# Windowed attention and two MLPs on one core: how the first heads are loaded, split and scored, and what TensorE does beside them

## The chip, the core and the metric

The kernel runs on one core of one Trainium2 chip. The core has TensorE (matrix products; its rows in the profile are PE, and PEld for its weight loads), VectorE (DVE), ScalarE (ACT), GpSimd (POOL) and SyncE (SP, which here issues the transfers between HBM and the on-chip memory). The metric is the time of one execution on the device in microseconds, as the median of several runs.

## The reference

Causal attention in a window of 128 positions with a slope per head, then two MLPs. Batch 4, 8 heads, 576 positions, head dimension 64; 2304 tokens of 512 columns; hidden size 2048.

```python
scores = scale * np.matmul(q, k.transpose(0, 1, 3, 2))
rel = pos[:, None] - pos[None, :]
bias = slopes[:, None, None] * (-np.abs(rel))[None, :, :]
mask = (rel >= 0) & (rel < 128)
scores = np.where(mask, scores + bias[None], -1000000000.0)
attn = softmax(scores)                       # with 1e-9 added to the sum
x = np.matmul(attn, v)                       # -> (2304, 512)
h = x @ w_in1;  x = where(h >= 1, h, where(h <= -1, 0, (h + 1)**2 / 4)) @ w_out1
h = x @ w_in2;  out = (h * np.clip(h + 3, 0, 6) / 6) @ w_out2
```

q, k and v are float32, the MLP weights float64.

## The kernel before

Products run in a rounded float32 type. For accuracy a factor is split into a rounded high part ("hi", `split_hi`) and the rest ("lo", `split_lo`), and a product is the sum of two or three partial products. Float64 weights arrive as words and are converted on the chip: `Weights.conv1` (ScalarE, two instructions), `conv2` (VectorE, three), `conv3` (ScalarE rounds, VectorE subtracts). One conversion serves one f, a slice of 128 of the 2048 hidden columns, with its w_in and w_out. `W1.load()` issues the next half (w_in, then w_out) of the next f on SP; `conv_tick` issues the second part of one conversion and the first part of the next.

The tokens are cut into nine units of 128 to 320; a unit has 8 heads, a head one step per 128 queries. Unit 0 has 256 tokens and so 16 steps, unit 1 has 320 and 24, unit 2 has 192 and 16. `tick` issues one step: `stage_a` (scores, bias and row extreme, exponential), and for earlier steps `stage_b` (transposes of the probabilities, p to t to th), `stage_c_whole` (product with v into r, normalising) and `stage_d_whole` (transpose into x, split). The first three units (`WHOLE`) take this form with unsplit probabilities; later units normalise ahead of the transposes and multiply in split form.

For each head `load` fetches keys and queries, 64 rows, twice, into both halves of the 128 partitions (kr, qr; two buffers each). `prep` splits: kh and kl hold hi and lo of the keys in both halves, and qs holds the queries' hi in its first 64 partitions and their lo in the last 64 (L286 rounds all 128 on POOL, L288 subtracts on POOL). So one product with kh over 128 rows gives hi times hi plus lo times hi, and two (L321, L322) make a score. v comes for two heads at a time, with a column of ones on either side for the row sums.

`make_consts` builds distances (rel) and a mask on POOL; `make_bias` makes each of the eight heads' bias on VectorE at the head's first step, from both. It also makes the identity for the transposes.

The program starts with `n_pre` = 20 ticks, which cover unit 0, with a load of a weight half at every third tick and a `conv_tick` at the last two. Then blocks 0 and 1 of 256 tokens each run the first half of the f (chunks of `Mlp1.first`, 12 products into h, L522, and `second`, 12 products into acc, L562), and then the second half; a hook between chunks issues weight loads, conversions and ticks of units 1 and 2 (`spread`). From then on the MLP's products fill the kernel, with the later units' steps between them.

SP issues its transfers in the order written (`manual_schedule`). For the other engines a planner chooses the order of instructions ahead of time from costs, so an engine's order can differ from the order of the code; each engine then executes its list in order.

Of the kernel before, what the change touches and what calls it, by code (L numbers as in the profile page):

```python
# [2 lines left out]

# [6 lines left out]
F32 = mybir.dt.float32  # L10
# [7 lines left out]
P = 128  # L18
# [7 lines left out]
F64_HI_TO_F32 = 2.0 ** -112  # L26


HI = dict(k="act", q="act", q_whole="pool", v="any", th="act", xf="act", x="act", g="act", x2="act")
LO = dict(k="any", q="pool", v="pool", x="any", x_whole="dve", g="pool", g_tail="dve", g2="dve", x2="dve")  # L30

LAG = 2
LAG_TAIL = 4
LAG_B, LAG_C, LAG_C_SPLIT, LAG_D = 2, 3, 4, 4
WHOLE = 3


@with_exitstack
def tile_window_attention_two_mlps(
# [53 lines left out]

    ident = const.tile([P, P], F32, tag="ident", name="ident")

    rel_mask = []

    def make_consts():
        both = cpool.tile([P, 2, PIECE], F32, tag="m", name="both")
        irel, mask = both[:, 0, :2 * P], both[:, 1, :2 * P]  # L100
        rel_mask.extend((irel, mask))

        nc.gpsimd.iota(irel, pattern=[[-1, 2 * P]], base=P, channel_multiplier=1,
                       allow_small_or_imprecise_dtypes=True)
        nc.gpsimd.memset(mask, 0.0)
        nc.gpsimd.affine_select(out=mask, in_=mask, compare_op=ALU.is_ge, fill=NEG / scale,
                                base=P, pattern=[[-1, 2 * P]], channel_multiplier=1)
        nc.gpsimd.affine_select(out=mask, in_=mask, compare_op=ALU.is_ge, fill=NEG / scale,
                                base=WINDOW - 1 - P, pattern=[[1, 2 * P]], channel_multiplier=-1)
        make_identity(nc, ident)  # L110
# [21 lines left out]
    class Weights:  # L132
# [47 lines left out]
            split_lo("dve", hl[:, 1], m, hl[:, 0])  # L180
            self.hl[f] = hl

        def conv_tick(self):
# [12 lines left out]
        def w_in(self, part, c, f):  # L196
# [5 lines left out]

    class Head:
        pass

    heads = []
    for j, (t0, n) in enumerate(units):
        for h in range(H):  # L210
            u = Head()
            u.unit, u.h, u.t0 = j, h, t0
            u.b, u.q0 = divmod(t0, S)
            u.nq = n
            u.q1 = u.q0 + n
# [5 lines left out]
            u.whole = j < WHOLE  # L221
            u.n_a = u.n_c = 0
            u.prepped = False
            heads.append(u)
# [6 lines left out]
    class Attention:  # L231
# [5 lines left out]
        def load(self, n):  # L237

            u = heads[n]
            u.kr = self.raw.tile([P, KMAX], F32, tag="kr", name=f"kr{n}")  # L240
            u.qr = self.raw.tile([P, UMAX], F32, tag="qr", name=f"qr{n}")
            self.k_owners.append(n)
            for dst, src, a, m in ((u.kr, kT, u.k0, u.nk), (u.qr, qT, u.q0, u.nq)):
                for r in range(2):
                    nc.sync.dma_start(out=dst[r * D:(r + 1) * D, :m], in_=src[u.b, u.h, :, a:a + m])
            if u.h % 2 == 0:
                self.v_owners.append(n)
                u.vt = self.raw.tile([P, KCH, 2 * D + 2], F32, tag="vr", name=f"vr{n}")
                u.vr = u.vt[:, :, 1:2 * D + 1]
                if u.whole:  # L250
# [12 lines left out]

        def may_load(self, n):

            if n >= len(heads):
                return False
            if len(self.k_owners) > 1 and not heads[self.k_owners[-2]].prepped:
                return False
            if heads[n].h % 2 == 0 and len(self.v_owners) > 1:  # L270
                o = self.v_owners[-2]
                if heads[o].whole and heads[o + 1].n_c < len(heads[o + 1].qbs):
                    return False
                if not heads[o].prepped:
                    return False
            return True

        def prep(self, n):
            u = heads[n]
            u.prepped = True  # L280
            u.kh = self.proc.tile([P, KMAX], F32R, tag="kh", name=f"kh{n}")
            u.kl = self.proc.tile([P, KMAX], F32R, tag="kl", name=f"kl{n}")
            u.qs = self.proc.tile([P, UMAX], F32R, tag="qs", name=f"qs{n}")
            m, nk = u.nq, u.nk
            split_hi(HI["k"], u.kh[:, :nk], u.kr[:, :nk])
            split_hi(HI["q_whole" if u.whole else "q"], u.qs[:, :m], u.qr[:, :m])  # L286
            split_lo(LO["k"], u.kl[:, :nk], u.kr[:, :nk], u.kh[:, :nk])
            split_lo(LO["q"], u.qs[D:, :m], u.qr[D:, :m], u.qs[D:, :m])  # L288
            if u.whole:
                return  # L290
            if u.h % 2 == 0:

                u.vs = self.proc.tile([P, 2, KCH, 2, D], F32R, tag="vs", name=f"vs{n}")
                full, rest = divmod(nk, P)
                parts = [(slice(0, P), slice(0, full))]
                if rest:
                    parts.append((slice(0, rest), slice(full, full + 1)))
                for pp, cc in parts:
                    for j in range(2):
                        src = u.vr[pp, cc, j * D:(j + 1) * D]  # L300
                        hi, lo = u.vs[pp, j, cc, j, :], u.vs[pp, j, cc, 1 - j, :]
                        split_hi(HI["v"], hi, src)
                        split_lo(LO["v"], lo, src, hi)
            else:
                u.vs = heads[n - 1].vs

        def stage_a(self, n, i):
# [21 lines left out]
            nc.scalar.activation(out=pt[:m, :nk], in_=pt[:m, :nk], func=AF.Exp, bias=sm[:m, 0:1],  # L329
                                 scale=-1.0, accum_out=None if u.whole else sm[:m, 1:2])  # L330
# [369 lines left out]
    with ExitStack() as actx:  # L700
# [3 lines left out]
        proc = actx.enter_context(tc.tile_pool(name="proc", bufs=2))  # L704
        work = actx.enter_context(tc.tile_pool(name="work", bufs=2))
        bias8 = actx.enter_context(tc.tile_pool(name="bias", bufs=1)).tile([P, H, 2 * P], BF16, tag="bias8", name="bias8")
        att = Attention(raw, proc, work, xs)

        att.more_loads(1)
        W1.load()  # L710
        make_consts()
# [12 lines left out]

        def spread(part, ticks, conv):
# [4 lines left out]
            def hook(f, after):  # L730
                k = 2 * (f - part[0]) + after + 1
                W1.load()
                while W1.n_conv < conv0 + min(conv, -(-conv * k // slots)) and W1.conv_tick():
# [122 lines left out]
```

## Time and profile before

| what | value |
|---|---|
| median of 3 runs | 1015.49 us (1014.09 to 1015.96) |
| profiled execution, its own time | 1019.89 us |
| its span, first to last instruction | 1018.1 us |
| mean granted TensorE clock over the span | 0.987 |
| TensorE (PE) busy | 984.6 us, 97% |
| VectorE (DVE) busy | 600.9 us, 59% |
| ScalarE (ACT) busy | 520.7 us, 51% |
| GpSimd (POOL) busy | 252.9 us, 25% |
| moved by DMA | 78.50 MB, mean 77 GB/s |

The median is of runs without the profiler. The profiled execution is a run of its own; its durations and windows add up to its own span. Busy shares are means over the whole span, and stages differ much.

### The profile page before, as it was taken

How to read it: one execution, taken by the hardware profiler on the slowest of the kernel's cores; microseconds unless marked ns; L12 is line 12 of the kernel's file. 1: busy time of each engine (PE TensorE's matmuls, PEld its weight loads, DVE VectorE, ACT ScalarE, POOL GpSimd, SP SyncE). 2: the span in 40 equal slices, each digit the busy share in tenths (PEclk: the TensorE clock that was granted, in tenths of full speed). 3: DMA queues.
4: the chain of work that ended last, by engine and by line, in shares of the span. 5: the costliest groups of instructions: out<-in, count | busy, mean ns of one | idle time of the engine just before them, and what ended most of it. 6: DMA issues, size and time to landing. Idle time of an engine off the chain costs nothing.

```text
span 1018.1 us, 17964 instructions
## 1 busy us (share of the span) xinstructions
PE 984.6 (97%) x6380; PEld 899.3 (88%) x6380; DVE 600.9 (59%) x1583; ACT 520.7 (51%) x1286; POOL 252.9 (25%) x398
## 2 busy tenths in 40 slices
PE   5898999999999999999999999999999999999998
PEld 4787888999989999999999999999988888888886
DVE  5778998566678676677757997922242223222222
ACT  4768875455677666566645777522242223222221
POOL 3334356444556555465410000000000000000000
PEclk9979999999999999999999999999999999999999
DMA  6565542311323211322005566000020002001001
GB/s 177 146 215 186 181 151 78 99 56 43 91 57 100 77 40 47 88 66 77 2 22 177 203 212 217 1 1 1 1 104 1 0 1 83 1 1 42 1 1 42
DMA packets 69785, 78.50 MB, mean 77 GB/s; under 512 B 7488, under 2 KB 61760, under 8 KB 69696
## 3 DMA queue, kind: packets, MB, share of 16 engines
q1 hardware_dynamic: 69696, 77.36, 24.4%
q8 instruction: 50, 0.82, 0.3%
q14 instruction: 39, 0.32, 0.1%
HBM read 66.85 MB, written 10.49 MB: 76 GB/s over the span
## 4 chain that ended last, share of the span: by engine, by line
PE 77%; DVE 4%; ACT 2%; issue 1%; POOL 1%; DMA 1%; SPq 0%; ACTq 0%; POOLq 0%
PE h L522 35%; PE acc L615 19%; PE acc L562 16%; PE r L441 2%; PE s L321 1%; PE t L355 1%; PE s L322 1%; PE t L356 1%; DVE r L549 0%; DMA rawb<-w_out 0%; DVE ma L173 0%; DVE p L326 0%; DVE r L551 0%; ACT r L550 0%; POOL g L128 0%
## 5 line engine op out<-in xcount | busy, mean ns | idle before, releaser
L522 PE MATMUL h<-x,wa 128*128 128x256 f32 x1728 | 246.2, 290 | 1.1 <-DVE wa L128 1.1
L562 PE MATMUL acc<-g,wa 128*128 128x256 f32 x1728 | 234.7, 284 | 2.0 <-POOL g L128 1.7
L522 PEld LDWEIGHTS h<-x,wa 128*128 128x128 f32 x1728 | 226.3, 197 | 2.3 <-DVE wa L128 1.5
L562 PEld LDWEIGHTS acc<-g,wa 128*128 128x128 f32 x1728 | 217.7, 191 | 3.8 <-POOL g L128 2.5
L522 PE MATMUL h<-x,wb 128*128 128x512 f32 (+1 forms) x960 | 210.5, 368 | 0.2 <-DVE r L605 0.2
L615 PE MATMUL acc<-wb,g 128*128 128x512 f32 x864 | 209.4, 390 | 0.0
L522 PEld LDWEIGHTS h<-x,wb 128*128 128x128 f32 x960 | 176.2, 188 | 25.5 <-DVE r L605 0.5
L615 PEld LDWEIGHTS acc<-wb,g 128*128 128x128 f32 x864 | 161.7, 188 | 32.4
L605 DVE SCALAR_TENSOR_TENSOR r<-r,h 128x512 f32<-128x512 f32 (+1 forms) x80 | 50.7, 634 | 201.2 <-ACT r L604 201.1
L604 ACT ACTIVATE r<-h 128x512 f32<-128x512 f32 (+1 forms) x80 | 44.5, 556 | 209.6 <-PE h L522 209.6
L121 ACT CAST g<-r 128x256 fp32r<-128x256 f32 (+2 forms) x224 | 104.3, 466 | 84.0 <-DVE r L605 49.8
L128 POOL TENSOR_TENSOR g<-r,g 128x256 fp32r<-128x256 f32 x112 | 90.4, 808 | 142.3 <-ACT g L121 128.1
L550 ACT ACTIVATE r<-r 128x256 f32<-128x256 f32 x144 | 60.0, 417 | 79.9 <-DVE r L549 76.7
L128 DVE TENSOR_TENSOR g<-r,g 128x512 fp32r<-128x512 f32 (+2 forms) x112 | 64.5, 576 | 46.8 <-ACT g L121 46.7
L329 ACT ACTIVATE p<-p,sm 128x256 f32<-128x256 f32 (+2 forms) x160 | 76.2, 477 | 23.8 <-DVE sm L326 21.7
L551 DVE TENSOR_TENSOR r<-h,r 128x256 f32<-128x256 f32 x144 | 60.6, 421 | 29.7 <-ACT r L550 28.6
L549 DVE TENSOR_SCALAR r<-h 128x256 f32<-128x256 f32 x144 | 60.3, 418 | 28.3 <-PE h L522 23.8
L128 POOL TENSOR_TENSOR qs<-qr,qs 64x256 fp32r<-64x256 f32 (+3 forms) x72 | 68.0, 946 | 24.5 <-issue 10.4
L326 DVE CUSTOM_DVE_ANT_0 p<-s,bias 128x256 f32<-128x256 f32 (+2 forms) x160 | 59.8, 375 | 21.0 <-PE s L322 20.1
L321 PE MATMUL s<-kh,qs 128*128 128x256 f32 (+2 forms) x160 | 57.1, 358 | 12.9 <-POOL qs L128 11.1
L334 POOL TENSOR_SCALAR p<-p,sm 128x256 f32<-128x256 f32 (+2 forms) x104 | 49.3, 474 | 54.2 <-DVE sm L333 35.1
L356 PE MATMUL t<-ident,p 128*128 128x128 f32 (+1 forms) x160 | 45.9, 287 | 3.5 <-ACT p L329 2.3
(71 smaller groups left out, 1112.3 us busy)
## 6 DMA issues: line engine op xcount, KB each, us to landing
rawa<-w_in SPq DMA_DIRECT2D x16, 512.0 KB, 5.3
rawa<-w_out SPq DMA_DIRECT2D x16, 512.0 KB, 5.0
rawb<-w_in SPq DMA_DIRECT2D x16, 512.0 KB, 3.7
rawb<-w_out SPq DMA_DIRECT2D x16, 512.0 KB, 4.7
x2d<-o SPq DMA_DIRECT2D x22, 256.0 KB, 2.2
kr<-kT SPq DMA_DIRECT2D x48, 112.0 KB, 2.6
out<-o SPq DMA_DIRECT2D x18, 256.0 KB, 2.2
kr<-kT SPq DMA_DIRECT2D x64, 64.0 KB, 2.2
```

The source lines that it names most:

```text
L121: nc.scalar.copy(hi, x)
L128: engines[eng].tensor_tensor(out=lo, in0=x, in1=hi.bitcast(F32), op=ALU.subtract)
L321: nc.tensor.matmul(ps[:m, :nk], u.qs[:, qo:qo + m], u.kh[:, ko:ko + nk], start=True, stop=False)
L326: nc.vector.tensor_tensor_reduce(out=pt[:m, :nk], in0=ps[:m, :nk], in1=bias8[:m, u.h, bo:bo + nk], scale=-scale, scalar=3.0e38, op0=ALU.ad ...
L329: nc.scalar.activation(out=pt[:m, :nk], in_=pt[:m, :nk], func=AF.Exp, bias=sm[:m, 0:1], scale=-1.0, accum_out=None if u.whole else sm[:m, ...
L356: nc.tensor.transpose(ps[:m, 1, :m], pt[:m, po:po + m], ident[:m, :m])
L522: nc.tensor.matmul(ps[:, :n], self.W.w_in(a, c, f), self.x_chunk(x, b, c, n), start=(k == 0), stop=(k == 3 * KC - 1))
L549: nc.vector.tensor_scalar(out=r[:, :n], in0=ps[:, :n], scalar1=-1.0, scalar2=1.0, op0=ALU.max, op1=ALU.min)
L550: nc.scalar.activation(out=r[:, :n], in_=r[:, :n], func=AF.Square, bias=0.5, scale=0.5)
L551: nc.vector.tensor_tensor(out=r[:, :n], in0=ps[:, :n], in1=r[:, :n], op=ALU.max)
L562: nc.tensor.matmul(acc[i][:, o * n:(o + 1) * n], self.W.w_out(a, f)[:, e * P:(e + 1) * P], g[:, b, :n], start=(first and k == 0 and o == 0 ...
L615: nc.tensor.matmul(acc[t][:, :DM], g[:, b, t * P:(t + 1) * P], self.W.w_out(a, f), start=(first and k == 0), stop=(last and k == 2))
```

## The change

Four things are changed in the first part of the program. In unit 0 (`PAIRS = 1`) the keys of two heads are loaded once, one head in partitions 0 to 63 and the other in 64 to 127, and so are the queries; the hi and lo parts are whole tiles (kh, kl, qh, ql), and a score is four products over 64 rows in place of two over 128. Queries are rounded on VectorE there instead of POOL. Unit 0's v goes to a tile of its own in the place of the last weight. The mask is folded into the distances, and all eight biases are made ahead of the first step, each as one product with the slope. TensorE gets products of zeros: 14 of 512 columns at the start, and one of 256 columns ahead of each score in the first three units, into the same bank, which the score then overwrites. The times at which the first ticks load and convert weights move (`LOAD_AT`, `CONV_AT`), and the planner is told to place `conv1` behind the last exponential issued and the first ticks behind the fifth bias. A copy of one zero on ScalarE comes first of all on that engine.

```diff
-HI = dict(k="act", q="act", q_whole="pool", ...)
-LO = dict(k="any", q="pool", v="pool", ...)
+HI = dict(k="act", q="act", q_pair="dve", q_whole="pool", ...)
+LO = dict(k="any", k_pair="dve", q="pool", q_pair="pool", v="pool", ...)
+WARM_UP = 14
+PAIRS = 1
+LOAD_AT = (1, 4, 7, 10, 13, 16, 19)
+CONV_AT = (9, 15)
...
+    def keep_busy(bank, n):
+        nc.tensor.matmul(bank[:, :n], zeros[:, :P], zeros[:, :n], start=True, stop=True, skip_group_check=True)
...
-        nc.gpsimd.memset(mask, 0.0)
-        nc.gpsimd.affine_select(out=mask, in_=mask, compare_op=ALU.is_ge, fill=NEG / scale,
+        nc.gpsimd.affine_select(out=rel, in_=rel, compare_op=ALU.is_ge, fill=-NEG / min(slopes),
...
-    def make_bias(h):
-        nc.vector.scalar_tensor_tensor(out=bias8[:, h, :], in0=rel_mask[0], scalar=-slopes[h] / scale,
-                                       in1=rel_mask[1], op0=ALU.mult, op1=ALU.add)
+        return [nc.vector.tensor_scalar(out=bias8[:, h, :], in0=rel, scalar1=-slopes[h] / scale, scalar2=None,
+                                        op0=ALU.mult) for h in range(H)]
...
             if n < KF:
-                self.conv1(n)
+                with tc.issue_after(after.ins) if after else nullcontext():
+                    self.conv1(n)
...
+            if not u.pair or u.h % 2 == 0:
...
+                    if u.pair:
+                        nc.sync.dma_start(out=dst[:, :m],
+                                          in_=src[u.b, u.h:u.h + 2, :, a:a + m].rearrange("h d m -> (h d) m"))
+                        continue
...
+                    if n == 0:
+                        self.first_v = wpool.tile([P, H // 2, u.nk // P, 2 * D + 2], F32, tag=f"w{KF - 1}", name="first_v")
+                        nc.gpsimd.memset(self.first_v[:, :, :, 0:2 * D + 2:2 * D + 1], 1.0)
...
+    def prep_pair(self, u, n):
...
+            split_hi(HI["k"], u.kh[:, :nk], u.kr[:, :nk])
+            split_hi(HI["q_pair"], u.qh[:, :m], u.qr[:, :m])
+            split_lo(LO["k_pair"], u.kl[:, :nk], u.kr[:, :nk], u.kh[:, :nk])
+            split_lo(LO["q_pair"], u.ql[:, :m], u.qr[:, :m], u.qh[:, :m])
+
+        def scores(self, u, ps, qo, ko, m, nk):
+            if u.pair:
+                d = slice(u.h % 2 * D, (u.h % 2 + 1) * D)
+                parts = [(q[d], k[d]) for k in (u.kh, u.kl) for q in (u.qh, u.ql)]
+            else:
+                parts = [(u.qs, u.kh), (u.qs, u.kl)]
+            for w, (q, k) in enumerate(parts):
+                nc.tensor.matmul(ps[:m, :nk], q[:, qo:qo + m], k[:, ko:ko + nk],
+                                 start=(w == 0), stop=(w == len(parts) - 1))
...
-            if n < H and i == 0:
-                make_bias(n)
...
-            nc.tensor.matmul(ps[:m, :nk], u.qs[:, qo:qo + m], u.kh[:, ko:ko + nk], start=True, stop=False)
-            nc.tensor.matmul(ps[:m, :nk], u.qs[:, qo:qo + m], u.kl[:, ko:ko + nk], start=False, stop=True)
+            if u.whole:
+                keep_busy(ps, 2 * P)
+            self.scores(u, ps, qo, ko, m, nk)
...
-        att.more_loads(1)
+        nc.vector.memset(zeros, 0.0)
+        nc.scalar.copy(zeros[:, 0:1], nc.const_aps.tensor(0.0, [P, 1], F32))
+        bank = psum.tile([P, BANK], F32, tag="h1", name="busy")
+        for _ in range(WARM_UP):
+            keep_busy(bank, BANK)
+        att.more_loads(3)
...
-            att.tick()
-            if t % 3 == 0:
+            with tc.issue_after(bias[H // 2].ins):
+                att.tick()
+            if t in LOAD_AT:
                 W1.load()
-            if t >= n_pre - 2:
-                W1.conv_tick()
+            if t in CONV_AT:
+                W1.conv_tick(att.exp)
```

## Rows read from the trace of the kernel before

**Rows 1.** Windows by stage: busy us (instructions) by engine, clock, DMA share, GB/s.

```profile
core 0: us, PE busy (x) PEld busy (x) DVE busy (x) ACT busy (x) POOL busy (x), PEclk, DMA share, GB/s
0.00:9.40 9.40, 0.00 (x1) 0.01 (x1) 2.70 (x6) 2.09 (x3) 3.77 (x16) 1.00 0.41 117
9.40:43.30 33.90, 29.62 (x122) 25.68 (x123) 24.14 (x67) 22.03 (x49) 9.81 (x18) 1.00 0.59 171
43.30:46.70 3.40, 2.48 (x16) 1.75 (x15) 3.33 (x10) 2.49 (x5) 1.43 (x3) 1.00 0.73 230
46.70:63.80 17.10, 16.67 (x75) 14.40 (x74) 8.32 (x30) 9.61 (x26) 4.19 (x7) 0.50 0.70 209
63.80:91.10 27.30, 24.20 (x176) 20.27 (x174) 24.98 (x58) 22.17 (x53) 12.83 (x13) 1.00 0.59 190
91.10:110.60 19.50, 17.37 (x112) 15.45 (x113) 16.59 (x43) 15.08 (x34) 6.51 (x9) 0.85 0.43 124
...
180.00:538.00 358.00, 352.95 (x2904) 344.27 (x2904) 249.70 (x896) 222.46 (x706) 175.82 (x293) 1.00 0.21 60
...
680.00:1018.10 338.10, 334.22 (x1515) 281.68 (x1513) 95.33 (x146) 85.90 (x148) 0.00 (x0) 1.00 0.06 21
```

**Rows 2.** Groups of TensorE's instructions, 10 to 41 us: count, busy us, mean ns.

```profile
L322 PE MATMUL s<-kl,qs 128*128 128x256 f32 x8 | 3.7, 460 | 0.0
```

**Rows 3.** The same, 47 to 63.5 us.

```profile
L322 PE MATMUL s<-kl,qs 128*128 128x256 f32 x5 | 2.1, 415 | 0.0
```

**Rows 4.** The same, 180 to 400 us.

```profile
L322 PE MATMUL s<-kl,qs 128*128 128x256 f32 x46 | 12.8, 279 | 0.0
```

**Rows 5.** Chain of waits, late in unit work: start us, us, what.

```profile
522.14 4.45 PE acc L562 x36
```

**Rows 6.** Timeline of the first 10 us: start us, us, engine, what.

```profile
0.73 1.20 SPq L245 DMA_DIRECT2D kr<-kT  x2
...
3.59 1.28 ACT L121 ACT_TABLE_LOAD   x1 [3.59 <-DMA kr<-kT]
...
8.57 1.64 POOL L128 TENSOR_TENSOR qs<-qr,qs 64x256 fp32r<-64x256 f32 x2
...
9.40 0.47 PE L321 MATMUL s<-kh,qs 128*128 128x128 f32 x1 [9.40 <-POOL qs L128]
```

**Rows 7.** Timeline of SP, 44 to 110 us.

```profile
50.59 0.58 SPq L154 DMA_DIRECT2D rawa<-w_out  x1
```

**Rows 8.** Timeline of ScalarE, 45 to 67 us.

```profile
61.70 1.13 ACT L162 ACTIVATE ma<-rawa 128x1024 f32<-128x1024 f32 x1
```

**Rows 9.** The page's DMA issues: count, KB each, median us to landing.

```profile
kr<-kT SPq DMA_DIRECT2D x48, 112.0 KB, 2.6
```

**Rows 10.** Groups of VectorE's instructions, 0 to 110.6 us.

```profile
L169 DVE TENSOR_SCALAR ma<-ma 128x1024 uint32<-128x1024 uint32 x9 | 6.7, 749 | 0.6 <-ACT ma L162 0.6
...
L113 DVE SCALAR_TENSOR_TENSOR bias<-both 128x256 bf16<-128x256 f32 x8 | 4.4, 599 | 0.0
...
L128 DVE TENSOR_TENSOR kl<-kr,kh 128x256 fp32r<-128x256 f32 x8 | 3.4, 423 | 7.2 <-ACT kh L121 7.1
...
L326 DVE DVE_READ_ACCUMULATOR2_ANT sm<- 128x1 f32 x34 | 2.8, 82 | 0.0
```

**Rows 11.** Groups of TensorE's instructions, 0 to 110.6 us.

```profile
L386 PE MATMUL r<-vr,th 128*64 128x65 f32 x16 | 2.9, 271 | 0.1
L386 PE MATMUL r<-vr,th 64*64 64x65 f32 x16 | 2.9, 267 | 0.0
```

**Rows 12.** Windows to 43.3 us of the tiles p, rec, x, th, each alone.

```profile
0.00:43.30 43.30, 8.25 (x23) 4.57 (x24) 5.60 (x16) 7.16 (x16) 0.00 (x0) 1.00 0.55 159
...
0.00:43.30 43.30, 2.29 (x9) 1.00 0.55 159
...
0.00:43.30 43.30, 6.72 (x24) 5.49 (x24) 1.27 (x3) 1.12 (x3) 1.00 0.55 159
...
0.00:43.30 43.30, 11.47 (x42) 10.33 (x42) 0.00 (x0) 4.68 (x15) 1.00 0.55 159
```

**Rows 13.** Window to 110.6 us of the tile ma: VectorE, ScalarE, clock, DMA.

```profile
0.00:110.60 110.60, 38.26 (x34) 19.85 (x18) 0.90 0.57 170
```

More of the change, by code (lines that the diff above doesn't have):

```diff
@@ L1 @@
 import math
-from contextlib import ExitStack
+from contextlib import ExitStack, nullcontext
 import concourse.bass as bass
@@ L181, in conv3, with conv_tick @@
             self.hl[f] = hl
-        def conv_tick(self):
+        def conv_tick(self, after=None):
             n = self.n_conv
@@ L239, in load @@
             u = heads[n]
[L240 to L245, printed above, removed]
-            if u.h % 2 == 0:
-                self.v_owners.append(n)
-                u.vt = self.raw.tile([P, KCH, 2 * D + 2], F32, tag="vr", name=f"vr{n}")
+            if not u.pair or u.h % 2 == 0:
+                u.kr = self.raw.tile([P, KMAX], F32, tag="kr", name=f"kr{n}")
+                u.qr = self.raw.tile([P, UMAX], F32, tag="qr", name=f"qr{n}")
+                self.k_owners.append(n)
+                for dst, src, a, m in ((u.kr, kT, u.k0, u.nk), (u.qr, qT, u.q0, u.nq)):
+                    if u.pair:
+                        nc.sync.dma_start(out=dst[:, :m],
+                                          in_=src[u.b, u.h:u.h + 2, :, a:a + m].rearrange("h d m -> (h d) m"))
+                        continue
+                    for r in range(2):
+                        nc.sync.dma_start(out=dst[r * D:(r + 1) * D, :m], in_=src[u.b, u.h, :, a:a + m])
+            if u.h % 2 == 0:
+                if u.unit == 0:
+                    if n == 0:
+                        self.first_v = wpool.tile([P, H // 2, u.nk // P, 2 * D + 2], F32, tag=f"w{KF - 1}", name="first_v")
+                        nc.gpsimd.memset(self.first_v[:, :, :, 0:2 * D + 2:2 * D + 1], 1.0)
+                    u.vt = self.first_v[:, n // 2]
+                else:
+                    self.v_owners.append(n)
+                    u.vt = self.raw.tile([P, KCH, 2 * D + 2], F32, tag="vr", name=f"vr{n}")
                 u.vr = u.vt[:, :, 1:2 * D + 1]
-                if u.whole:
+                if u.whole and u.unit > 0:
                     nc.gpsimd.memset(u.vt[:, :, 0:2 * D + 2:2 * D + 1], 1.0)
@@ L267, in may_load @@
                 return False
-            if len(self.k_owners) > 1 and not heads[self.k_owners[-2]].prepped:
+            takes = not heads[n].pair or heads[n].h % 2 == 0
+            if takes and len(self.k_owners) > 1 and not heads[self.k_owners[-2]].prepped:
                 return False
-            if heads[n].h % 2 == 0 and len(self.v_owners) > 1:
+            if heads[n].h % 2 == 0 and heads[n].unit > 0 and len(self.v_owners) > 1:
                 o = self.v_owners[-2]
@@ L280, in prep @@
             u.prepped = True
+            if u.pair:
+                self.prep_pair(u, n)
+                return
             u.kh = self.proc.tile([P, KMAX], F32R, tag="kh", name=f"kh{n}")
@@ L305, in prep @@
                 u.vs = heads[n - 1].vs
+        def prep_pair(self, u, n):
+            if u.h % 2:
+                first = heads[n - 1]
+                u.kh, u.kl, u.qh, u.ql = first.kh, first.kl, first.qh, first.ql
+                return
+            m, nk = u.nq, u.nk
+            u.kh = self.proc.tile([P, KMAX], F32R, tag="kh", name=f"kh{n}")
+            u.kl = self.proc.tile([P, KMAX], F32R, tag="kl", name=f"kl{n}")
+            u.qh = self.proc.tile([P, UMAX], F32R, tag="qs", name=f"qh{n}")
+            u.ql = self.proc.tile([P, 2, KCH, 2, D], F32R, tag="vs", name=f"ql{n}")
+            u.ql = u.ql.rearrange("p j c a d -> p (j c a d)")[:, :UMAX]
+            split_hi(HI["k"], u.kh[:, :nk], u.kr[:, :nk])
[3 more added lines that the diff above has]
+        def scores(self, u, ps, qo, ko, m, nk):
+            if u.pair:
+                d = slice(u.h % 2 * D, (u.h % 2 + 1) * D)
+                parts = [(q[d], k[d]) for k in (u.kh, u.kl) for q in (u.qh, u.ql)]
+            else:
+                parts = [(u.qs, u.kh), (u.qs, u.kl)]
+            for w, (q, k) in enumerate(parts):
+                nc.tensor.matmul(ps[:m, :nk], q[:, qo:qo + m], k[:, ko:ko + nk],
+                                 start=(w == 0), stop=(w == len(parts) - 1))
         def stage_a(self, n, i):
             u = heads[n]
-            if n < H and i == 0:
-                make_bias(n)
             a, m = u.qbs[i]
@@ L328, in stage_a @@
                 scalar=3.0e38, op0=ALU.add, op1=ALU.min, accum_out=sm[:m, 0:1])
-            nc.scalar.activation(out=pt[:m, :nk], in_=pt[:m, :nk], func=AF.Exp, bias=sm[:m, 0:1],
-                                 scale=-1.0, accum_out=None if u.whole else sm[:m, 1:2])
+            self.exp = nc.scalar.activation(out=pt[:m, :nk], in_=pt[:m, :nk], func=AF.Exp, bias=sm[:m, 0:1],
+                                            scale=-1.0, accum_out=None if u.whole else sm[:m, 1:2])
             if not u.whole:
@@ L706, in tile_window_attention_two_mlps @@
         bias8 = actx.enter_context(tc.tile_pool(name="bias", bufs=1)).tile([P, H, 2 * P], BF16, tag="bias8", name="bias8")
+        zeros = actx.enter_context(tc.tile_pool(name="zeros", bufs=1)).tile([P, BANK], BF16, tag="zeros", name="zeros")
         att = Attention(raw, proc, work, xs)
-        att.more_loads(1)
+        nc.vector.memset(zeros, 0.0)
[4 more added lines that the diff above has]
+        att.more_loads(3)
         W1.load()
-        make_consts()
+        bias = make_consts()
         new_x(0)
@@ L732, in hook @@
                 W1.load()
-                while W1.n_conv < conv0 + min(conv, -(-conv * k // slots)) and W1.conv_tick():
+                while W1.n_conv < conv0 + min(conv, -(-conv * k // slots)) and W1.conv_tick(att.exp):
                     pass
```

19 lines of the change are left out of this document (9 added, 10 removed).

## The prediction

> **What bounds the kernel now.** I read the windows view first, cut into stages [rows 1]. TensorE is busy for 352.95 of the 358.0 us from 180 us on, and for 334.22 of the last 338.1, and the diff touches nothing there: what the change is worth lies ahead of 180 us, and since the tail is TensorE's with hardly a gap, whatever the head saves or loses reaches the end one for one.
>
> What the reader is to see in the head is how the engines change places. Up to 9.4 us TensorE has done one instruction. Then, to 43.3 us, it is busy 29.62 of 33.9 us, more than VectorE (24.14) or ScalarE (22.03). Then comes a stretch (46.7 to 63.8 us) where it is busy 16.67 of 17.1 us and VectorE only 8.32, and after it VectorE leads: 24.98 of 27.3 us, a share of 0.915, and 16.59 of 19.5 us, 0.851.
>
> The clock column needs care. It says 0.50 for 46.7 to 63.8 us, the lower level (1.2 GHz), and 1.00 for 0 to 43.3 us; but no change of level is recorded up to 43.3 us, so that 1.00 is no reading. Durations are one: the second score product with 256 columns takes 460 ns on the mean between 10 and 41 us [rows 2], 415 ns in the slow stretch [rows 3], and 279 ns between 180 and 400 us [rows 4]. So TensorE ran at the lower level for all of unit 0 too, though busy 87% of it. A 256-column product at the upper level costs 4.45 us / 36 = 124 ns in an unbroken row [rows 5]. All kinds mixed, one costs 29.62 / 122 = 243 ns from 9.4 to 43.3 us and 24.20 / 176 = 137 ns from 63.8 to 91.1 us [rows 1].
>
> Last, the start and the queue in order of time. ScalarE loads its function table only when the first keys land, at 3.59 us; the second query split ends at 10.2 us and the first score starts at 9.4 us, behind the first one's split [rows 6]. Weights come late: the w_out piece of f = 3 is issued at 50.59 us [rows 7], and its conversion begins on ScalarE at 61.70 us [rows 8]. Between 46.7 and 63.8 us VectorE, which does most of a conversion, has little to do.
>
> **A: the first score, 9.4 us now.** SP issued five transfers for the first head, at 1.20 us for two [rows 6]; now one for two heads' keys and one for their queries come first, 0.6 us each, so queries should land near 0.73 + 1.2 + 2.6 = 4.5 us (2.6 us to landing for the nearest size, 112 KB [rows 9]). VectorE rounds them (the lo part of keys in the same shape takes it 0.42 us [rows 10]; a copy is at most that) and the first product needs no lo part, so the data allow some 4.9 us. But the 14 products of zeros stand ahead on TensorE. They wait for a memset and for ScalarE's table load, 1.28 us [rows 6], so they start near 2.2 us. No row has a bf16 product of 512 columns; from 256 columns, twice 124 ns [rows 5] gives 3.5 us for fourteen, twice 243 ns (the price of all kinds) 6.8 us. So they end between 5.7 and 9.0 us; with the level rising on the way, 6.9. Worth -2.5 us (-0.4 to -3.7).
>
> **B: unit 0, 33.9 us now.** TensorE: the 112 products of the unit (32 score, 32 transposes, 48 with v) become 160, since each score takes four products of 64 rows and there are 16 of zeros. Half the rows save no time: the product with v takes 267 ns on 64 rows and 271 ns on 128 [rows 11]. At the upper level 160 x 137 ns = 22.0 us [rows 1]. VectorE, by the tiles' own windows up to 43.3 us [rows 12]: 5.60 us for the 16 score rows, and 16 x 0.08 us for reading out their extremes [rows 10]; normalising, 2.29 us for three of four pairs, so 3.1; lo parts of x, 1.27 for three, so 1.7; four lo parts of keys at 0.42, 1.7; four roundings of queries, of which no row stands, taken at 0.3 each (0.2, as a one-operand row gives below, to 0.42), 1.2: together 14.6 us. A conversion of a weight costs it 38.26 us / 34 x 4 instructions = 4.5 us [rows 13]; with one of them 19.1. ScalarE [rows 12, 13]: 7.16 us of exponentials, 4.68 / 15 x 16 = 5.0 of copies of transposes, 1.5 of x, four roundings of keys (1.6, at 0.4 each as an estimate from x's 1.12 / 3), and some five of the conversions' instructions at 19.85 / 18 = 1.1 each: 20.8 us. Three engines near 20 us, each fed by the others in order, don't overlap wholly: at a share of 0.85 for TensorE's 22.0 I get 26 us, **-7.9**; at VectorE's best share, 0.915, it is 24.0 (-9.9), and at its present one (24.14 / 33.9 = 0.71) 31 (-2.9). The gain hangs on the upper level: it is the rival below if that isn't held.
>
> Fewer transfers count here: 32 issues at 0.58 us become 8, 14 us of SP's time, and half the bytes. I give that no term of its own; its worth is that weights queued behind come earlier, which C uses. POOL loses eight roundings and four lo parts; it is idle most of this stretch (9.81 of 33.9 us busy), so nothing.
>
> **C: from unit 0's end to 110.6 us, 67.3 us now**, where VectorE's work sets the pace once it isn't starved. Its work to 110.6 us is 2.70 + 24.14 + 3.33 + 8.32 + 24.98 + 16.59 = 80.1 us [rows 1]. The change takes off four lo parts of keys (1.7) and, on the biases, 4.4 us for eight two-operand instructions [rows 10], for which eight one-operand ones come: the nearest one takes 0.75 us for 1024 columns, 0.19 for 256, 1.6 in all, so -2.8. It adds 1.2 of query rounding: 76.8. Of these some 2.5 come before the first score and 19.1 in unit 0; 55.2 remain, including some 1.5 conversions that today run inside unit 0 and that the new order puts behind its last exponential. At the mean share of 63.8 to 110.6 us, 41.57 / 46.8 = 0.888, that takes 62.2 us: **-5.1**. The starved stretch is what goes: eight loads of weights are issued by unit 0's last steps, and unit 0 ends some 10 us earlier. At today's share of the whole stretch (53.2 / 67.3 = 0.79) it would be 69.9, +2.6; at 0.915, 60.3, -7.0.
>
> **D: 40 products of zeros in units 1 and 2**, 124 ns each [rows 5] at the most, 5.0 us. In unit 1 VectorE is behind most waits, so part of TensorE's time there is free; each also sits in the chain through the one score bank. Between 0 and +5.0 I take half, +2.5. In return they may hold the level between 91.1 and 110.6 us, where its mean is 0.85 now; I count nothing for it.
>
> The separate tile for unit 0's v (the last weight's place) removes waits of SP's for buffers but its reader, weight f = 15, loads after 100 us; nothing.
>
> **Sum:** -2.5 - 7.9 - 5.1 + 2.5 = -13.0 us. The profiled execution took 1019.89 us (span 1018.1, 1.8 us around it), so 1006.9 on its own scale; it lies 4.4 us above the median of the runs, 1015.49, and on that scale I say 1002.5 us. The best ends together give -20.6 (995), the worst +4.3 (1020).
>
> **Rivals.**
>
> *The level is lost again in unit 0* (slower). The warm-up raises the clock, and scores, transposes and exponentials at their pace don't hold it. For it: the same kinds of work, busy 87%, didn't raise it in 34 us [rows 1 to 3], and when it had risen at 43.3 us it fell again at 46.7 with TensorE busy for 0.73 of the time between. Then 160 products x 243 ns = 38.9 us, at 0.87 busy 44.7 us instead of 33.9: +10.8 in B, with A -2.5, C 0 (the slow stretch stays) and D +2.5 or more: about +11, 1026 us; lost halfway through the unit, it is about 1015, so that is the point from which it decides. Against: from 63.8 to 91.1 us, with unit 1's steps and few other products (176 in 27.3 us), it stayed at the upper level. The Trainium skill, "TensorE: Matmul & The Clock Gate", Part 4, says that transposes don't count as activity for the clock as other products do. By that rule a third of unit 0's old work counts for nothing, which would fit its low level; but the new score and zero products make up much more of the mix, 80 of 160. No run so far shows which wins. Chance 0.13.
>
> *Conversions stay the brake.* Unit 0 gets shorter, but the weights' conversions, now later in the order, keep VectorE waiting as today: A -2.5, B between -7.9 and -2.9, C +2.6, D +2.5 to +5.0: 1010 to 1022 us, most likely 1013. For it: 1.5 conversions move behind unit 0 and the loads of unit 1 still wait in SP's queue for buffers. Against: the DMA engines are busy only 0.59 of 9.4 to 43.3 us, so there is room to come earlier. Chance 0.15.
>
> *More than that.* VectorE at 0.915 all along, no fall of the clock, zeros hidden: -18 to -20, 996 us. Chance 0.2.
>
> *The transfers and biases were hidden and only the clock matters* changes little of the sum, since B rests on the clock; it isn't a case of its own. The remaining 0.52 is the forecast, 998 to 1009 us.
>
> **Range and chances.** 990 to 1016 us leaves out most of the first rival and the upper part of the second. Runs of this kernel differ by about 0.2% (2 us), so faster means under 1013.5: forecast, third rival and about half of the second, 0.80; same 0.08; slower 0.12.
>
> **What would show it.** A: the first score near 7 us. B: score products of 256 columns near 280 ns, and unit 0's last exponential near 33 us. C: no stretch between 40 and 65 us with VectorE under half busy, a fourth conversion begun before 50 us, and the 96th product of h (the end of block 0's first half) near 95 us in place of 110.6. D: zero products of 124 ns or less, and no stretch at 0.50 between 45 and 110 us. It is wrong if the clock falls inside unit 0, if VectorE's share after it stays at 0.79, or if the order of the engines' work is rearranged later in the kernel so that TensorE has gaps after 180 us.

## The result and the profile after

The changed kernel takes 1027.89 us (median of 4 runs, 1026.92 to 1030.01) against 1015.73 us beside it: a ratio of 1.0116, interval 1.0082 to 1.0151. It is slower by some 12 us, where 13 us faster was forecast. Its profiled execution took 1027.52 us, span 1025.7, and lies at its median; that of before lay 4 us above its own, so the two spans differ by 7.6 us only, and the traces can place no more than that of the 12. The ratios below leave out executions more than 1.5% above the fastest of the same kernel, which are five of the ten of run e16 and none of any other.

The windows of the changed kernel, with columns as in [rows 1], and one of the kernel before to set beside the fourth row:

```profile
0.00:7.50 7.50, 5.23 (x17) 2.04 (x17) 3.27 (x13) 2.29 (x4) 3.65 (x14) 1.00 0.68 198
7.50:12.80 5.30, 4.99 (x34) 3.90 (x32) 2.47 (x10) 2.91 (x8) 0.73 (x1) 1.00 1.07 357
12.80:42.20 29.40, 28.77 (x111) 22.16 (x111) 11.50 (x42) 12.66 (x31) 4.14 (x5) 0.50 0.36 102
42.20:117.20 75.00, 64.57 (x422) 56.23 (x421) 58.36 (x140) 52.17 (x116) 24.39 (x30) 0.83 0.47 148
...
180.00:538.00 358.00, 352.89 (x2901) 343.92 (x2901) 249.28 (x901) 222.58 (x710) 179.88 (x300) 1.00 0.22 63
```

```profile
42.90:110.60 67.70, 61.13 (x378) 52.26 (x378) 53.62 (x138) 49.55 (x116) 24.96 (x32) 0.83 0.58 178
```

The tail is as before. 42.2 us is the end of unit 0's last exponential (42.9 before, by the timeline), 117.2 us the end of the 96th product of h (110.6 before). From its first score to its last exponential unit 0 takes 34.7 us (33.5 before, from 9.4 us), so it gave back most of the 1.9 us that the start won; the stage after it lost 7.3 us, and what follows it 1.0. The third row is the one to read: the level falls at 12.8 us and stays at 0.50 through unit 0, with TensorE busy 28.77 of 29.40 us and VectorE 11.50. TensorE is the bound there, at half its rate: 28.77 / 111 = 259 ns for a product of any kind. The kernel before ran unit 0 at that level too, as its durations show ([rows 2] against [rows 4]); the clock of its first 43.3 us is no reading. So the level lost here is lost against the forecast and not against the kernel before.

TensorE's timeline at the start, and its groups from 13 to 42 us (compare [rows 4]; the zeros' first line stands for all fourteen):

```profile
2.27 5.01 PE L103 MATMUL busy<-zeros 128*128 128x512 bf16 x14 [2.27 <-ACT zeros L761]
...
7.54 0.32 PE L354 MATMUL s<-kh,qh 64*128 64x128 f32 x1
```

```profile
L103 PE MATMUL s<-zeros 128*128 128x256 bf16 x12 | 4.9, 408 | 0.6 <-DVE sm L375 0.6
...
L354 PE MATMUL s<-kl,qh 64*128 64x256 f32 x6 | 2.5, 412 | 0.0
```

The zeros at the start did raise the level: fourteen took 5.01 us, and the first score starts at 7.54 us, with products of 128 columns at 110 ns spacing; to 12.8 us a product takes 4.99 / 34 = 147 ns. What followed did not keep it. Weights past the third are later, not earlier: SP issues the fourth weight's w_in at 51.30 us (41.53 before), and its conversion begins at 64.93 us (61.70 before [rows 8]). The first three conversions begin later too, at 26.9, 43.2 and 51.7 us against 21.1, 29.6 and 38.9. SP's line after and before, then ScalarE's after:

```profile
51.30 0.59 SPq L154 DMA_DIRECT2D rawa<-w_in  x1
```

```profile
41.53 0.59 SPq L150 DMA_DIRECT2D rawa<-w_in  x1
```

```profile
64.93 1.13 ACT L166 ACTIVATE ma<-rawa 128x1024 f32<-128x1024 f32 x1
```

### The profile page after: what moved, and what is told of

Read it like the earlier page. It is cut to its first block, busy times and chain, and to the rows that moved or that the text cites. A ratio compares the mean times of both kernels' runs of the same rounds, so it can differ in the third digit from the quotient of the medians.

```text
span 1025.7 us, 18083 instructions
## 1 busy us (share of the span) xinstructions
PE 998.6 (97%) x6482; PEld 905.8 (88%) x6482; DVE 596.8 (58%) x1584; ACT 519.6 (51%) x1283; POOL 243.7 (24%) x382
## 4 chain that ended last, share of the span: by engine, by line
PE 84%; DVE 5%; ACT 4%; DMA 3%; issue 2%; POOL 1%; SPq 1%; ACTq 0%; DVEq 0%; POOLq 0%
PE h L571 36%; PE acc L664 19%; PE acc L611 16%; PE s L354 4%; PE r L490 2%; PE r L435 2%; PE t L404 2%; PE t L405 1%; DMA kr<-kT 1%; SPq L258 1%; POOL g L132 1%; DVE kl L132 1%; DVE ma L175 1%; PE s L103 1%; DVE r L598 1%
## 5 line engine op out<-in xcount | busy, mean ns | idle before, releaser
L571 PE MATMUL h<-x,wa 128*128 128x256 f32 x1728 | 243.1, 288 | 2.2 <-DVE wa L132 1.5
L611 PE MATMUL acc<-g,wa 128*128 128x256 f32 x1728 | 238.4, 286 | 5.3 <-POOL g L132 3.7
L571 PEld LDWEIGHTS h<-x,wa 128*128 128x128 f32 x1728 | 222.9, 194 | 4.1 <-DVE wa L132 1.9
L132 POOL TENSOR_TENSOR qs<-qr,qs 64x320 fp32r<-64x320 f32 (+3 forms) x64 | 61.9, 968 | 25.1 <-issue 10.5
L354 PE MATMUL s<-kh,qs 128*128 128x256 f32 (+2 forms) x144 | 51.0, 354 | 1.1 <-DVE sm L375 0.6
L417 DVE TENSOR_TENSOR tl<-t,th 128x256 fp32r<-128x256 f32 (+2 forms) x120 | 41.7, 348 | 11.6 <-ACT th L125 10.3
```

The source lines that it names most:

```text
L132: engines[eng].tensor_tensor(out=lo, in0=x, in1=hi.bitcast(F32), op=ALU.subtract)
L354: nc.tensor.matmul(ps[:m, :nk], q[:, qo:qo + m], k[:, ko:ko + nk], start=(w == 0), stop=(w == len(parts) - 1))
L571: nc.tensor.matmul(ps[:, :n], self.W.w_in(a, c, f), self.x_chunk(x, b, c, n), start=(k == 0), stop=(k == 3 * KC - 1))
L611: nc.tensor.matmul(acc[i][:, o * n:(o + 1) * n], self.W.w_out(a, f)[:, e * P:(e + 1) * P], g[:, b, :n], start=(first and k == 0 and o == 0 ...
```

## The experiments

Four theories were told apart. Theory 1: the level is lost, and unit 0's additional products cost at the lower one. Theory 2: the conversions' later order costs. Theory 3: the zeros cost their own time. Theory 4, formed later: the stage with unit 1 is long because the level falls in it too. The lines below are edits of the kernel named. The clock is the median over a kernel's runs of the mean granted clock, the before kernel's own runs beside these reaching 0.984 to 0.997. Those values are too high to set beside the others: no change of level is recorded in the kernel before ahead of 43.3 us, so unit 0's 33.9 us at half rate aren't counted. By that window they are worth 33.9 / 2 / 1018.1 = 0.017 of the mean (an estimate), which would take the profiled 0.987 to 0.970, against 0.973 for the changed kernel.

| kernel | us, median | ratio to before (interval) | clock |
|---|---|---|---|
| changed | 1027.9 | 1.0116 (1.0082 to 1.0151) | 0.974 |
| e1 heads loaded singly | 1020.5 | 1.0044 (1.0018 to 1.0071) | 0.980 |
| e2 no zeros at scores | 1019.8 | 1.0035 (1.0002 to 1.0067) | 0.975 |
| e3 before, zeros alone | 1013.6 | 0.9990 (0.9960 to 1.0021) | 0.984 |
| e4 old conversions | 1022.7 | 1.0068 (1.0052 to 1.0085) | 0.978 |
| e5 more zeros, unit 0 | 1022.2 | 1.0062 (1.0030 to 1.0095) | 0.988 |
| e6 no order asked | 1030.3 | 1.0144 (1.0129 to 1.0159) | 0.974 |
| e7 e1 and e4 | 1018.8 | 1.0037 (1.0016 to 1.0057) | 0.981 |
| e8 e5 and e4 | 1028.7 | 1.0135 (1.0118 to 1.0152) | 0.976 |
| e9 more zeros, units 0 and 1 | 1014.9 | 0.9980 (0.9961 to 0.9998) | 0.995 |
| e10 e1, products repeated | 1014.0 | 0.9984 (0.9968 to 1.0000) | 0.988 |
| e11 e3 and biases | 1010.9 | 0.9955 (0.9939 to 0.9971) | 0.990 |
| e12 e3, more zeros | 1011.9 | 0.9968 (0.9950 to 0.9985) | 0.995 |
| e13 e9 and e4 | 1022.2 | 1.0063 (1.0037 to 1.0089) | 0.978 |
| e14 e11, more zeros | 1011.3 | 0.9963 (0.9941 to 0.9986) | 0.996 |
| e15 e11 and v's place | 1018.9 | 1.0032 (1.0009 to 1.0055) | 0.982 |
| e16 v as before | 1030.5 | 1.0092 (1.0046 to 1.0139) | 0.973 |
| e17 e1, half-height repeat | 1024.8 | 1.0083 (1.0050 to 1.0116) | 0.976 |
| e18 e11 and pairs | 1026.5 | 1.0106 (1.0044 to 1.0167) | 0.973 |

**e1, heads loaded singly.**

```diff
-PAIRS = 1
+PAIRS = 0
```

> The changed kernel with every head loaded for itself and two score products over 128 rows in place of four over 64; zeros, biases, v and the order of conversions stay. Theory 1 (TensorE at the lower level through unit 0, with 32 products more, is what costs): 32 products of about 0.21 us go, some 7 us at the lower level; unit 0's last exponential near 36 us in place of 41.7, time 1018 to 1021 us, and if products over all rows also keep the level up, 1010 or less. Theory 2 (the conversions' later order costs): time stays at 1025 to 1028 us. Theory 3 (the zeros cost): the same, 1025 to 1028.

1020.5 us: 7 us of the 12 come with the pairs. The level was lost here too, from 12.3 us on, but came back within unit 0 for some 7 us (19.0 to 25.9). The window from its first score to unit 0's last exponential:

```profile
7.10:37.70 30.60, 24.52 (x124) 20.41 (x121) 19.98 (x64) 16.40 (x45) 11.39 (x21) 0.70 0.62 174
```

**e2, no zeros at scores.**

```diff
-            if u.whole:
-                keep_busy(ps, 2 * P)
```

> The changed kernel without the 56 products of zeros ahead of scores; the 14 at the start stay. Theory 1: the 16 in unit 0 cost 0.21 us each at the lower level, 3.4 us, and those in units 1 and 2 up to 5 us, so 1020 to 1025 us, unless the level is lost sooner and more often, 1028 to 1035. Theory 2: no change but for the up to 5 us of the later ones, 1023 to 1028. Theory 3: most of the loss goes, 1016 to 1020.

1019.8 us, faster than the changed kernel by 8 us, with the same clock: 256 columns of zeros per score didn't hold the level, and cost. That lies in the range of Theory 3 and 0.2 us below that of Theory 1, so it doesn't part the two. The expectation's own prices (16 x 0.21 and 40 x 0.12 us at the most) make 8.2 us. How they fall is seen in the changed kernel's timeline, first in unit 0, then in unit 1:

```profile
22.02 0.42 PE L103 MATMUL s<-zeros 128*128 128x256 bf16 x1
...
22.37 0.47 PE L354 MATMUL s<-kh,qh 64*128 64x128 f32 x1
```

```profile
96.61 0.28 PE L103 MATMUL s<-zeros 128*128 128x256 bf16 x1
...
96.65 0.36 PE L354 MATMUL s<-kh,qs 128*128 128x256 f32 x1
```

In unit 0 at the lower level the next product starts 0.22 to 0.35 us behind the zeros, in unit 1 mostly 0.03 to 0.1.

**e3, the kernel before with zeros alone.** `keep_busy`, its tile, the 14 at the start and the one ahead of each score are added as in the change.

> The kernel before with the zeros alone: 14 at the start and one ahead of each score in the first three units. Theory 1: the first score is not earlier (data at 9.4 us), the level rises at the start and falls again in unit 0 before 20 us; with 16 x 0.21 us more work at the lower level 1016 to 1021 us; if the level holds for most of unit 0, 1005 to 1010. Theory 3: 1020 or more. Theory 2: 1013 to 1018, since the order of conversions is the old one.

1013.6 us; its interval holds no change. So zeros aren't bad in themselves: with singly loaded heads and the old order they cost nothing that the runs resolve.

**e4, conversions and loads as before** (e6 takes the last two lines alone; e7 adds `PAIRS = 0`, e8 the edit of e5).

```diff
-LOAD_AT = (1, 4, 7, 10, 13, 16, 19)
-CONV_AT = (9, 15)
+LOAD_AT = (0, 3, 6, 9, 12, 15, 18)
+CONV_AT = (18, 19)
...
-                W1.conv_tick(att.exp)
+                W1.conv_tick()
...
-                while W1.n_conv < conv0 + min(conv, -(-conv * k // slots)) and W1.conv_tick(att.exp):
+                while W1.n_conv < conv0 + min(conv, -(-conv * k // slots)) and W1.conv_tick():
```

> The changed kernel with conversions and loads of weights at the old ticks, and no order asked of their first parts; all else of the change stays. Theory 2 (the later order of the conversions costs, since it leaves them to be done after unit 0): the third conversion ends before 52 us in place of 65.6, block 0's first half ends near 111 us in place of 117.2, time 1014 to 1020 us. Theory 1 (four half-height products and zeros at the lower level cost): unit 0 stays at the lower level and gets longer with conversions in it, time 1024 to 1029 us.

> The changed kernel with the new ticks for loads and conversions, but the conversions' first parts not ordered behind the last exponential. Theory 2, if the order asked for is what makes them late: 1014 to 1020 us, as with the old ticks. If the ticks matter and not the order, 1024 to 1029. Theory 1: 1024 to 1029.

> The changed kernel with every head loaded for itself (two score products over 128 rows) and conversions and loads of weights as in the kernel before; the zeros, the biases as one product and v in its own place stay. If pairing and the conversions' order hold the whole loss, this is as fast as the old kernel with zeros alone, 1010 to 1015 us; if the biases or the place of v cost something, 1016 or more.

> The changed kernel with two products of zeros of 512 columns ahead of each score of unit 0 (which held the upper level there) and conversions and loads as in the kernel before. If what ate the gain of the held level was the conversions' order, 1008 to 1014 us, block 0's first half done near 105 us; if unit 1's stage is slow for another reason, 1018 or more, and its products at the lower level for long stretches as before.

1022.7 us for e4, but not as Theory 2 has it: conversions go back into unit 0, which then lasts to 51.4 us at the lower level, and the stage after it takes 62.2 us in place of 75.0:

```profile
8.30:51.40 43.10, 39.45 (x152) 30.31 (x152) 20.54 (x59) 20.40 (x44) 4.71 (x6) 0.53 0.39 119
51.40:113.60 62.20, 57.83 (x417) 49.85 (x417) 52.93 (x136) 50.02 (x116) 20.76 (x29) 0.94 0.56 173
```

e6, 1030.3, is no better than the change. e8, 1028.7, lost the level that e5 holds. e7, 1018.8, is no faster than e1 beyond their intervals, and slower than e3, so something in biases or v's place cost.

**e5, more zeros in unit 0; e9, in units 0 and 1** (`u.unit <= 1`).

```diff
-            if u.whole:
+            if u.unit == 0:
+                keep_busy(ps, BANK)
+                keep_busy(ps, BANK)
+            elif u.whole:
                 keep_busy(ps, 2 * P)
```

> The changed kernel with two products of zeros of 512 columns ahead of each score of unit 0 in place of one of 256; units 1 and 2 as they were. Theory 1: if the level holds at the upper one through unit 0, its last exponential comes near 34 us and the time falls to 1008 to 1018 us in spite of 16 x 0.33 us more work; if it is lost all the same, 768 columns more per step at the lower level cost 16 x 0.64 = 10 us, 1035 to 1040. Theory 2: even with the upper level held the third conversion ends after 60 us and the time stays above 1020. Theory 3: 1030 or more with the level held.

> The changed kernel with two products of zeros of 512 columns ahead of each score of units 0 and 1 in place of one of 256. Theory 4 (after unit 0 the stage with unit 1 is long because TensorE falls to the lower level in it, 38.6 us with more zeros in unit 0 alone): the level holds in both, the stage from unit 0's last exponential to the 96th product of h takes 62 to 66 us in place of 81.9 and the time falls to 1006 to 1014 us. Theory 2 (the late conversions alone make it long): the stage stays above 72 us and the time above 1018 even where the level holds.

Windows of e5 and then e9, from the first score to unit 0's last exponential, and on to the 96th product of h:

```profile
9.30:36.00 26.70, 26.04 (x166) 18.24 (x166) 16.78 (x54) 15.82 (x41) 4.45 (x6) 1.00 0.53 157
36.00:117.90 81.90, 70.97 (x421) 61.45 (x419) 59.09 (x141) 52.65 (x118) 25.03 (x30) 0.76 0.42 136
```

```profile
8.90:35.60 26.70, 26.04 (x165) 18.25 (x165) 16.78 (x54) 15.81 (x41) 4.45 (x6) 1.00 0.57 172
35.60:106.90 71.30, 65.53 (x437) 53.37 (x436) 55.40 (x135) 50.66 (x112) 23.77 (x30) 0.93 0.49 157
```

With the level held, unit 0 takes 26.7 us, where 26 was forecast, though with 768 columns of zeros more per step than the forecast counts. But e5 loses it after unit 0 (0.76) and takes 81.9 us there. This profiled execution took 1030.8 us; e5's median is still 1022.2. e9 holds it (0.93) and is 13 us faster than the changed kernel, by adding work that does nothing. Theory 4 holds in direction. Yet 71.3 us is not the 62 to 66 expected, so Theory 2 keeps a part.

**e10 and e17, repeats of unit 0's score products with singly loaded heads**, into the unused half of the bank; e17 repeats over 64 rows (`u.qs[:D]`, `k[:D]`).

```diff
-PAIRS = 1
+PAIRS = 0
...
+            if u.unit == 0:
+                self.scores(u, ps[:, 2 * P:], qo, ko, m, nk)
             self.scores(u, ps, qo, ko, m, nk)
```

> The changed kernel with every head loaded for itself, and in unit 0 both score products over 128 rows issued twice, the first time into an unused half of the same bank. The number of products is the same as with pairs, but all are over 128 rows. If it is the number of products that costs: 1026 to 1030 us and about 29 us at the lower level in unit 0, as with pairs. If products over 64 rows keep the level less well: the lower level in unit 0 shrinks to 15 us or less, and the time to 1018 to 1022 us.

> The changed kernel with every head loaded for itself, and in unit 0 the two score products issued once more over the first 64 rows alone, into an unused half of the same bank. With the repeat over all 128 rows it was 1014.0 us, without any repeat 1020.5. If products over 64 rows keep the level less well: 1018 to 1024 us and more than 15 us at the lower level up to unit 0's end. If the number of products counts and not their height: 1012 to 1016 us and less than 10 us.

With whole repeats 1014.0 us, 6 us faster than without any; with half-height repeats of the same columns 1024.8. The two kernels issue the same number of products with the same columns, so it is their height that makes the difference. Where e17 loses the level isn't shown: its profiled execution took 1015.89 us at clock 0.988, the other nine 1020.8 to 1027.0 at 0.973 to 0.983, so no row of it stands here. e10's windows, cut as e9's:

```profile
7.90:35.00 27.10, 22.87 (x151) 19.32 (x150) 18.54 (x63) 16.44 (x44) 11.37 (x19) 0.86 0.70 201
35.00:102.10 67.10, 58.44 (x416) 50.11 (x414) 54.82 (x137) 51.59 (x116) 27.77 (x31) 0.93 0.64 188
```

**e11, e3 and the biases as one product each**, with `issue_after` on the first ticks; **e12**, e3 with two products of 512 zero columns per score in unit 0 and one in unit 1; **e14**, e11 with e12's zeros.

```diff
-        make_consts()
+        bias = make_consts()
...
-            att.tick()
+            with tc.issue_after(bias[H // 2].ins):
+                att.tick()
```

> The kernel before with the zeros, and the eight biases made as one product each ahead of the first step, the first ticks placed behind the fifth; v, conversions and loads as before. The kernel with zeros alone took 1013.6 us and the one with biases, v's own place and zeros 1018.8. If the biases' part makes that difference: 1016 to 1020 us; if v's place does: 1011 to 1015.

> The kernel before with 14 products of zeros at the start, two of 512 columns ahead of each score of unit 0, one of 512 in unit 1 and one of 256 in unit 2; nothing else of the change. Theory 4: the level holds from the start to 110 us and the time falls to 1003 to 1010 us. Theory 3 (zeros cost more than they give): 1016 or more.

> The kernel before with biases as one product each, 14 products of zeros at the start, two of 512 columns ahead of each score of unit 0, one of 512 in unit 1, one of 256 in unit 2. If the level still has something to give over the version with 256 columns (1010.9 us): 1004 to 1009 us. If the zeros' own time takes it back: 1010 to 1014 us.

e11, 1010.9 us, beats both kernels, by 0.45% over before. e12 and e14 hold more of the level (0.995, 0.996) and are no faster than e11; that the zeros' own time takes it back is the likely reading, as e14's second expectation has it, and isn't shown apart. e11's windows:

```profile
6.90:40.80 33.90, 26.41 (x138) 22.16 (x135) 23.82 (x70) 21.78 (x50) 11.00 (x23) 0.75 0.66 186
40.80:102.60 61.80, 57.38 (x408) 48.88 (x407) 52.98 (x138) 48.90 (x116) 24.47 (x32) 0.94 0.63 194
```

**e13, e9 with the old conversions** (e4's edit).

> The changed kernel with two products of zeros of 512 columns ahead of each score of units 0 and 1, and conversions and loads at the old ticks without an order asked. If the conversions' order holds what is left of the loss once the level is held: stage with unit 1 near 62 us, 1004 to 1010 us. If it doesn't: 1013 to 1018 us. If conversions inside unit 0 make the level fall there: 1020 or more, with the lower level in unit 0 for 20 us or more.

```profile
8.30:56.00 47.70, 43.60 (x165) 31.01 (x168) 24.35 (x62) 22.76 (x46) 4.97 (x6) 0.54 0.37 112
56.00:115.40 59.40, 58.81 (x416) 48.22 (x422) 50.41 (x133) 48.53 (x113) 24.68 (x29) 0.99 0.56 176
```

The third expectation came true: with conversions between its steps, paired unit 0 loses the level and lasts to 56.0 us; the stage after it is short at 59.4.

**e15, v's own place added to e11; e16, taken from the changed kernel.**

```diff
+                if u.unit == 0:
+                    if n == 0:
+                        self.first_v = wpool.tile([P, H // 2, u.nk // P, 2 * D + 2], F32, tag=f"w{KF - 1}", name="first_v")
...
-            if heads[n].h % 2 == 0 and len(self.v_owners) > 1:
+            if heads[n].h % 2 == 0 and heads[n].unit > 0 and len(self.v_owners) > 1:
```

> The kernel before with the zeros, the biases as one product each and v's own place for unit 0; loads and conversions as before. If v's place costs by sending keys and queries ahead of weights in SP's queue: the third weight's w_in is issued near 28 us in place of 21.2, the third conversion ends after 54 us in place of 45.2, and the time is 1016 to 1020 us in place of 1010.9. If it costs nothing, as forecast: 1009 to 1013 us.

> The changed kernel with unit 0's v in the two shared buffers as before. If v's place costs here too: 1018 to 1024 us in place of 1027.9. If with pairs the queue is short enough that it doesn't matter: 1025 to 1030 us.

e15 costs 8 us. SP's timeline, the third weight's w_in in e11 and then in e15:

```profile
21.17 0.43 SPq L149 DMA_DIRECT2D rawa<-w_in  x1
```

```profile
27.96 0.59 SPq L149 DMA_DIRECT2D rawa<-w_in  x1
```

Without the check on v's buffers, keys and queries of later heads are issued sooner, ahead of weights, and SP then stands at their buffers. e16 is inconclusive: 1015.3 us in one run and up to 1036.7 in others.

**e18, pairs added to e11 alone** (e16 with e4's edit). With the pairs come VectorE's rounding of their queries and one pair more loaded at the start.

> The fastest version so far (the kernel before with zeros and with the biases as one product each, 1010.9 us) with unit 0's keys and queries in pairs and four half-height products per score, and nothing else of the change. If pairing by itself loses the level in unit 0: 1018 to 1026 us, with TensorE at the lower level for 25 us or more before unit 0's last exponential. If pairing costs only with the late conversions: 1006 to 1013 us.

```profile
7.30:52.20 44.90, 40.46 (x154) 30.89 (x154) 20.58 (x59) 21.00 (x44) 4.24 (x7) 0.56 0.30 95
52.20:116.20 64.00, 58.81 (x413) 49.91 (x413) 52.53 (x136) 49.17 (x115) 26.93 (x31) 0.91 0.60 185
```

Pairing alone costs 15.5 us over e11, and unit 0 runs at a mean of 0.56 for 44.9 us against 0.75 for 33.9.

## Why the prediction was wrong, point by point

**The step that failed is B**, "at the upper level 160 x 137 ns". The changed kernel left the upper level at 12.8 us; from there to unit 0's end a product took 259 ns, and unit 0 took 34.7 us in place of 26. Where the level is held it takes 26.7 us (e5, e9), but that is no check of the sum: with their additional zeros TensorE is busy 26.04 us there and not 22.0, at a share of 0.98 and not 0.85.

My reasons against the first rival, to which I gave 0.13, were both bad. One was the stretch from 63.8 to 91.1 us, said to hold few products other than unit 1's steps. Its lines (64 to 91 us) show 78 of some 176 that are the MLP's, over all 128 rows, with 13.4 of 24.2 us busy:

```profile
L562 PE MATMUL acc<-g,wa 128*128 128x256 f32 x52 | 8.5, 295 | 1.1 <-POOL g L128 0.9 <-ACT g L121 0.2
...
L522 PE MATMUL h<-x,wa 128*128 128x256 f32 x26 | 4.9, 302 | 0.6 <-DVE wa L128 0.6
```

The other, that score and zero products are half of the new mix, took a product over 64 rows for as good as one over 128. It does take as long [rows 11], but e10 and e17 show that it doesn't keep the level as well. The pairing thus doubled the score products and weakened each (e18).

That rival named the place rightly, and its 1026 us is near the 1027.9 measured. The size is luck: it put +10.8 us on unit 0 and nothing on the stage behind it, where the traces have +1.2 and +7.3.

The Trainium skill's rule on transposes, that they don't count for the clock as other products do ("TensorE: Matmul & The Clock Gate", Part 4), points the way the run went; no run here varied the transposes, so it is neither shown nor refuted.

**C failed as well.** VectorE's work in the stage was sized well, 55.2 us forecast, 58.4 measured and 55.4 in e9; its share was not: 0.78 (58.4 / 75.0) in place of 0.888, and still 0.78 in e9 with the level near held. Where conversions come early, e11 has 52.98 / 61.8 = 0.86 and e13 0.85, with part of the conversions' work moved into unit 0. So VectorE alone doesn't pace this stage; late weights and a low level both go with a longer one. The late conversions were in the second rival, the level in this stage in neither. That rival's upper end, 1022 us, doesn't follow: its own worst terms (-2.5 - 2.9 + 2.6 + 5.0) give 1018 on the scale of its 1010, and 1022 only on that of the profiled execution.

**A** was right: first score at 7.5 us, forecast 6.9. The eight biases took 1.8 us; 1.6 was forecast, and they are a gain (e11 against e3: 2.6 us, at the edge of the intervals).

**D**, +2.5 us for the 40 zero products of units 1 and 2, stays untested: e2's 8 us are for all 56, and by the timeline those of unit 0 cost more each. **v's place** was set at nothing; with singly loaded heads it costs 8 us (e15), with pairs it stays open. The spread between runs was put at 2 us; the kernel before went from 1011.1 to 1021.8 us in 110 executions.

**What stays open:** how the 12 us divide. Taking out one part gives 7.4 us (pairs, e1), 8.1 (zeros at scores, e2) or 5.2 (the conversions' order, e4); these don't add up, since each also moves the level and the stage behind unit 0. Open too is whether a paired unit 0 with the level held and early conversions would win. e8 and e13 tried it and lost the level. How much of the stage's remaining length in e9 is the conversions' order and how much the place of the loads wasn't separated.

## What to carry to other kernels

A part that saves transfers and vector work can cost more through TensorE's clock than it saves: before counting a product at the fast level, ask which products will hold that level, and use windows with the granted clock for each stage of the trial. A trial in which useless whole-height work is added (e9, e10) is cheap and tells whether the clock is the matter, if every stage concerned gets it: e5, with zeros in unit 0 alone, held the level there and was still at 1022.2 us. A clock that shows 1.00 before its first recorded change has to be checked against durations. And a queue in written order has to be read for what a removed wait lets past: here keys and queries went ahead of weights.

## What the runs showed of the hardware

Over 110 executions of the kernel before, on the chips of these runs, the mean granted clock went from 0.984 to 0.997 and the time fell by 0.72 us for each 0.001 (a straight line, 1008.9 us at 1.000, with unit 0's time at the lower level in it). e16's ten runs have much the same slope, 0.74 us (1015.3 us at 0.995, 1022.7 at 0.983, 1036.7 at 0.965): the time of one program differs by over 20 us along with the level. In the changed kernel's unit 0 TensorE was busy 28.77 of 29.40 us and stayed at 0.50 throughout. bf16 products of zeros raised it: at the start of the changed kernel their weight loads come 0.43 us apart up to 6.04 us, then seven in 1.29 us. Whole-height repeats held it where half-height ones of the same columns did not (1014.0 against 1024.8 us, clock 0.988 against 0.976).
